# RWKV-6 with a SiLU MLP: a kernel's first unit turns its tokens in quarters of the array, spreads u from one row and copies level 1 in another order

## The chip, the cores and the metric

The kernel runs on one core of one Trainium2 chip. The metric is the device time of one execution in microseconds (us). Before the change the median of three runs is 566.68 us (566.24, 566.68 and 570.93). One execution was recorded by the hardware profiler: it took 566.43 us, of which 564.6 us lie between the first and the last instruction (its span). Times of single instructions below are counted from the start of that span.

Names of engines: PE is TensorE (PEld its weight load), DVE is VectorE, ACT is ScalarE, POOL is GpSimd, SP is SyncE. SPq and ACTq are the instruction queues of SP and ACT when they issue DMAs.

## What is computed

Batch 4, 8 heads, 768 tokens, head dimension 48; then an MLP from 384 to 2048 to 384. All data are float32.

```python
def _attn_ref(r, k, v, w, u):
    state = np.zeros((B, H, D, D))
    for t in range(S):
        kt, vt, rt, wt = k[:, :, t], v[:, :, t], r[:, :, t], w[:, :, t]
        cur = np.einsum('bhd,bhe->bhde', u[None] * kt, vt)
        y[:, :, t] = np.einsum('bhd,bhde->bhe', rt, state + cur)
        state = wt[:, :, :, None] * state + np.einsum('bhd,bhe->bhde', kt, vt)
    return y

def _moe_ref(x, w_in, w_out):          # x: (3072, 384), from y
    h = x @ w_in
    g = h * (1.0 / (1.0 + np.exp(-h)))
    return g @ w_out
```

A token's own key and value thus count with the weight u (the "bonus"), and older ones with the product of the decays w in between.

## The kernel before, in words

**Units.** The 768 tokens are cut into 6 stretches of 128 tokens (`L`), and the batch into pairs (`NB = 2`); one stretch of one pair is a unit, 12 in all. The order of the instructions on every engine is written out by hand: `do((fn, args), ...)` calls the steps one after the other, and each engine takes its own instructions in that order. The change touches the steps of unit 0 nearly alone; unit 1 shares some of its functions.

**Scores by levels.** Within a unit a 128 by 128 score matrix is built in 7 levels. Level l splits the tokens into blocks of `c = 2^l`: a query in an odd block meets the keys of the even block before it. For that, queries `tr`, keys `tk` and decays `tw` are needed with the head dimension on the partitions; between levels the queries and keys are multiplied on by products of decays (`grow_queries` on DVE, `grow_keys` on POOL, `product` mostly on POOL, `odd_keys` a copy on ACT). `score_products` on PE makes a level's scores in PSUM, and `keep_masked` (line 724 in the profile) copies them into `score` on DVE under a mask of int8, two copies of 128x512 for a level. At level 1 its pattern takes runs of two elements.

**First loads.** `load_tokens(0)` (line 111) fetches k, r and w of unit 0 into `raw`, each in two DMAs of 192 KB: the first batch element's tokens onto partitions 0 to 63 by SP's queue, the second's onto partitions 64 to 127 by ACT's queue. Each partition row holds two successive tokens. Behind them on SP's queue stand u, read once for every one of the 128 partitions (line 281), and the weights and later tokens.

**Turning.** `turn` (lines 357 to 390) brings tokens onto the columns with PE: a matmul by the identity. For each of the two tokens s of a row, `turn_in` issues 8 matmuls (4 head pairs p, 2 heads e) that contract over all 128 partitions; the 64-wide outputs of the two heads fill the upper and lower half of the PSUM partitions. An fp32 matmul stands in the trace as two instructions, so one `turn_in` shows as 16. `turn_out` copies the result into `tk`, `tr` or `tw` on ACT: for k in two copies of 128x256 (the second batch element reversed), else in one of 128x512. For w the order of s is reversed (`back`).

**Bonus.** `bonus(0, 0)` on POOL (line 442) multiplies r of a row's second token by k of its first; `bonus(0, 1)` on DVE (444) multiplies r by k of the same token, `bonus(0, 2)` (446) multiplies that by u, and `bonus_sum` (451, 455) reduces over the head dimension. `bonus_spread` brings the sums into place with PE, and `bonus_part(x)` (603) writes a quarter of them into `score`.

**First keys.** `start_keys(0, DVE, True)` and `(..., False)` (line 672) are four DVE products of 128x128 elements with steps of four elements. Behind them on DVE stand `grow_queries(0, 0)` (629) and `product(0, 0)` (416), and POOL's `grow_keys(0, 1)` (647) waits for the latter.

**Beats.** `beat(n)` issues n transposes of the identity on PE (line 1382) whose result nobody reads.

The DVE and ACT share the PSUM tile `p_w` of two banks for rounding the weights later on; in unit 0 the first bank takes the spread bonus, and the second is free.

Of the kernel before, what the change touches and what calls it, by code (L numbers as in the profile page):

```python
# [38 lines left out]
def kernel(  # L39
# [73 lines left out]

    def load_tokens(i):
        for name, src in (("k", k), ("r", r), ("w", w)):
            load_twos(twos(raw[:, i % NSLOT, WRK[name]])[0], src, i, [nc.sync, nc.scalar if i == 0 else nc.sync])

    def load_blocks(i, name, g):

# [152 lines left out]
    u_bc = const.tile([128, H, D], F32, name="u_bc")  # L272

    def load_u():
        for b in range(NB):
# [62 lines left out]
    own_mask = const.tile([128, NB, L // 2, 2], I8, name="own_mask")  # L338
    for b in range(NB):
        for x in range(2):  # L340
            nc.vector.tensor_single_scalar(out=own_mask[:, b, :, x:x + 1], in_=first[0], scalar=tok[:, x, b:b + 1],
                                           op=ALU.is_equal)
        for l in range(1, NL):
            nc.vector.tensor_single_scalar(out=masks[l][:, b], in_=first[l], scalar=tok[:, l, b:b + 1], op=ALU.is_equal)

    def clear_score():
        nc.gpsimd.memset(score, 0.0)
# [4 lines left out]
    def turn(i, b, name):  # L352
        dst = {"w": tw, "r": tr, "k": tk}[name]
        if i not in dst:
            rows = NX if name == "k" else Q
            t = pt.tile([128, rows, L], F32, name="t" + name, bufs=2 if name == "r" else 1)
            dst[i] = [t] if name == "w" else t
        t = dst[i][0] if name == "w" else dst[i]
        if i < NTOK:
            if (i, b, name) not in turned:  # L360
                turn_in(i, b, name)
# [9 lines left out]
    def turn_in(i, s, name):  # L371

        flat = raw[:, i % NSLOT, WRK[name]].rearrange("p b h d -> p (b h d)")
        p_tr = bank("p_sc" if (i, name) == (0, "r") else "p_m", NP, NB, L // 2)
        for p in range(NP):
            for e in range(2):
                at = ((2 * p + e) * 2 + s) * D
                nc.tensor.matmul(p_tr[PD * e:PD * e + PD, p].rearrange("p b i -> p (b i)"), lhsT=flat[:, at:at + PD],
                                 rhs=ident, start=(p == 0), stop=(p == NP - 1))
        turned[i, s, name] = p_tr  # L380

    def turn_out(i, s, name, t):
        p_tr = turned.pop((i, s, name))
        if name == "k":
            to = t[:, NP:].rearrange("p q (i s) -> p q i s", s=2)
            nc.scalar.copy(out=to[:, 0:NP, :, s], in_=p_tr[:, :, 0])
            nc.scalar.copy(out=to[:, NP:2 * NP, :, 1 - s], in_=p_tr[:, ::-1, 1, ::-1])
        else:
            to = t.rearrange("p (b q) (i s) -> p q b i s", b=NB, s=2)[:, :, :, :, s]
            nc.scalar.copy(out=to, in_=p_tr)  # L390

    def clear_rest():

# [34 lines left out]
    def bonus(i, x):  # L428
# [3 lines left out]
        if x == 0:  # L432
# [7 lines left out]
            if i == NTOK:  # L440
                ruk[i, 0] = spare[:, 0:H * D].rearrange("p (h d) -> p h d", h=H)
            engine.tensor_tensor(out=ruk[i, 0], in0=rk(i, 0)[:, :, 1], in1=rk(i, 1)[:, :, 0], op=ALU.mult)
# [222 lines left out]
    def start_keys(i, engine, own):  # L665

        n = NP * L // 4
        for b in range(NB):
# [3 lines left out]
            engine.tensor_tensor(out=keys(i, X[1] * L + 3 * b, [4, n], [1, 1]) if own else have, in0=have,  # L672
                                 in1=odd_products(i, 0, b, [4, n], skip=2 * x), op=ALU.mult)

    def start_levels(i):

        start_keys(i, nc.gpsimd, True)
# [43 lines left out]
    def keep_masked(i, l, e, sc):  # L721
        c, ni = 1 << l, L >> (l + 1)
        dst = score[:, i % NSC, e].rearrange("p (b q) (i s c) -> p b q i s c", b=NB, s=2, c=c)[:, :, :, :, 1, :]
        nc.vector.copy_predicated(out=dst, mask=masks[l][:, :, None].to_broadcast([128, NB, NP, ni, c]),  # L724
                                  data=sc[e].rearrange("p (b q) (i c) -> p b q i c", b=NB, c=c))

    def scores(i, l, *between):
        c, ni = 1 << l, L >> (l + 1)
# [665 lines left out]
    others = {1: [(beat, 6)], 2: [(turn, 1, 0, "r"), (head_weight, 0), (beat, 2), (bonus_part, 1)],  # L1394
              3: [(turn, 1, 1, "r"), (head_weight, 1), (beat, 2), (bonus_part, 2)], 4: [(turn, 1, 1, "w"), (reverse_v, 0), (bonus_part, 3)],
              5: [(turn, 1, 0, "w")], 6: [(turn_in, 1, 0, "k"), *blocks[0:4], (tail_weight, 0)]}
    for l in range(1, NL):
        do((scores, 0, l), *[(grow_keys, 0, l + 1)] * (l + 1 < NL), *others[l])

    do((bonus, 1, 0), (bonus, 1, 1), (product, 1, 0), (bonus, 1, 2), *both(x_products, 0), (join_weight, 0), (add_weight,),  # L1400
       (x_copy, 0, 0), (tail_weight, 1), (x_copy, 0, 1), (turn_apart, 0), (turn_in, 1, 1, "k"), *both(turn, 1, "k"), (join_weight, 1),
       (odd_ones, 1), (start_keys, 1, nc.gpsimd, True), (add_weight,), (tail_weight, 2), (head_weight, 2), (grow_queries, 1, 0),
       (up, 0, 0), (turn_k, 0), (join_weight, 2), *blocks[4:8],
       (start_keys, 1, nc.gpsimd, False), (add_weight,), (tail_weight, 3), (odd_keys, 1, 1), (head_weight, 3), (grow_keys, 1, 1),
# [93 lines left out]
```

## Time and profile before

| what | value |
|---|---|
| median of three runs | 566.68 us |
| profiled execution | 566.43 us, span 564.6 us |
| PE busy | 555.2 us (98%) |
| DVE busy | 477.3 us (85%) |
| POOL busy | 396.2 us (70%) |
| ACT busy | 272.0 us (48%) |
| PE busy from 5 to 65 us | 56.40 of 60 us |
| PE busy from 65 to 180 us | 114.99 of 115 us |
| PE's granted clock (page) | full in all 40 slices |
| DMA moved | 57.59 MB |

An engine's busy time is the time in which one of its instructions runs; a bracket such as [0.88 <-DVE tw L416] ahead of an instruction says how long its engine stood idle, and what ended that. In a line of the timeline "x32" stands for 32 instructions merged into one stretch. Matmuls overlap, so a matmul's own duration is longer than the distance to the next.

### The profile page before, as it was taken

The numbers are of one execution on the slowest core, as the hardware profiler recorded it, in microseconds if no ns is written. First come the engines' busy times: TensorE is split into PE (matmuls) and PEld (weight loads), VectorE is DVE, ScalarE is ACT, GpSimd is POOL, SyncE is SP. The second block draws the span as 40 slices with busy tenths as digits, with TensorE's granted clock in tenths as the row PEclk, the third lists the DMA queues.
The fourth block names the chain that finished last, engine by engine and source line by source line (L and its number), as shares of the span: only waits on it lengthen the run. The fifth ranks groups of instructions, "written<-read, shape, count | busy, mean of one in ns | idle before, by whom it ended". The sixth has DMA issues, their size and how long they took to land.

```text
span 564.6 us, 18890 instructions
## 1 busy us (share of the span) xinstructions
PE 555.2 (98%) x7782; PEld 516.8 (92%) x7782; DVE 477.3 (85%) x747; ACT 272.0 (48%) x618; POOL 396.2 (70%) x448
## 2 busy tenths in 40 slices
PE   8999999999999999999999999999999999999997
PEld 7777777699899989999999999999999999999997
DVE  7999798998999989999889889889889989882250
ACT  4679695452461372373374274274274272271330
POOL 6999898527789998969796696696696696700000
PEclk9999999999999999999999999999999999999999
DMA  9946886345445445265555554555555552102000
GB/s 221 311 80 189 241 252 106 46 78 116 104 76 87 106 78 96 56 133 95 106 96 97 118 87 90 118 86 92 115 84 97 115 88 61 39 4 57 29 9 21
DMA packets 206485, 57.59 MB, mean 102 GB/s; under 512 B 186048, under 2 KB 198208, under 8 KB 206400
## 3 DMA queue, kind: packets, MB, share of 16 engines
q1 hardware_dynamic: 203712, 54.23, 46.6%
q10 hardware_dynamic: 2688, 2.16, 1.6%
q8 instruction: 61, 1.00, 0.8%
q14 instruction: 24, 0.20, 0.1%
HBM read 47.14 MB, written 9.18 MB: 100 GB/s over the span
## 4 chain that ended last, share of the span: by engine, by line
PE 68%; POOL 12%; DVE 8%; DMA 4%; issue 3%; SPq 3%; ACT 1%; DVEq 0%; POOLq 0%
PE p_o L1339 22%; PE p_o L1193 13%; PE p_h L1193 9%; PE p_h L1086 4%; PE p_m L1275 4%; PE p_h L1339 4%; POOL tk L647 2%; PE p_sc L706 2%; PE p_sc L1339 2%; SPq L127 2%; POOL ruk L498 2%; PE p_m L870 2%; POOL tw L416 2%; POOL w_in_sb L1132 2%; DVE tr L629 2%
## 5 line engine op out<-in xcount | busy, mean ns | idle before, releaser
L647 POOL TENSOR_TENSOR tk<-tk,tw 128x256 f32<-128x256 f32 x112 | 88.6, 811 | 5.1 <-PE p_sc L706 1.5
L1339 PE MATMUL p_o<-own,temps 128*128 128x192 f32 x496 | 82.8, 326 | 0.0
L1339 PEld LDWEIGHTS p_o<-own,temps 128*128 128x128 f32 x496 | 80.9, 190 | 0.1
L1193 PE MATMUL p_o<-xt,w_in_sb 128*64 128x128 f32 x1152 | 72.3, 273 | 0.9 <-POOL w_in_sb L1132 0.7
L416 POOL TENSOR_TENSOR tw<-tw 128x256 f32<-128x256 f32 (+6 forms) x71 | 42.3, 595 | 38.2 <-DVE tw L366 34.8
L1086 PE MATMUL p_h<-xt,w_in_sb 128*128 128x256 f32 x288 | 66.3, 384 | 1.8 <-POOL w_in_sb L260 1.5
L1193 PEld LDWEIGHTS p_o<-xt,w_in_sb 128*64 128x64 f32 x1152 | 64.7, 137 | 1.3 <-POOL w_in_sb L1132 1.0
L1086 PEld LDWEIGHTS p_h<-xt,w_in_sb 128*128 128x128 f32 x288 | 53.5, 190 | 10.4 <-POOL w_in_sb L260 3.0
L498 POOL TENSOR_TENSOR ruk<-tokens_rk 128x384 f32<-128x384 f32 x48 | 54.3, 1152 | 9.3 <-DMA tokens_rk<-in_k_dram 9.3
L629 DVE TENSOR_TENSOR tr<-tr,tw 128x512 f32<-128x512 f32 x57 | 53.4, 937 | 1.1 <-PE p_m L706 0.4
L1339 PE MATMUL p_o<-w_out_sb,gt 128*128 128x192 f32 x292 | 51.7, 330 | 0.3 <-DVE ob L1347 0.3
L1339 PEld LDWEIGHTS p_o<-w_out_sb,gt 128*128 128x128 f32 x292 | 47.4, 190 | 1.5 <-DVE ob L1347 0.9
L656 POOL TENSOR_TENSOR tk<-tk,tw 128x256 f32<-128x256 f32 x32 | 25.1, 813 | 27.2 <-DVE tk L366 22.6
L1308 DVE TENSOR_TENSOR temps<-gt 128x512 f32<-128x512 f32 (+1 forms) x48 | 43.7, 948 | 0.0
L1344 ACT COPY partial<-p_o 128x192 f32<-128x192 f32 x32 | 10.2, 318 | 66.5 <-PE p_o L1339 64.7
L617 ACT COPY tk<-tk 128x256 f32<-128x256 f32 x52 | 20.9, 402 | 39.4 <-POOL tk L647 29.4
L1217 ACT ACTIVATE gt<-p_o 128x512 f32<-128x512 f32 x45 | 26.0, 602 | 23.1 <-PE p_o L1193 23.0
L1339 PE MATMUL p_h<-w_out_sb,gt 128*128 128x192 f32 x184 | 31.9, 326 | 0.0
L1339 PE MATMUL p_o<-w_out_sb,temps 128*128 128x192 f32 x176 | 30.5, 327 | 0.0
L1339 PEld LDWEIGHTS p_h<-w_out_sb,gt 128*128 128x128 f32 x184 | 30.2, 190 | 0.0
L724 DVE COPY_PREDICATED score<-mask,p_sc 128x512 f32<-128x512 int8 x38 | 28.4, 809 | 1.3 <-PE p_sc L706 1.3
L1339 PEld LDWEIGHTS p_o<-w_out_sb,temps 128*128 128x128 f32 x176 | 28.8, 190 | 0.3 <-ACT partial L1344 0.3
(258 smaller groups left out, 1314.6 us busy)
## 6 DMA issues: line engine op xcount, KB each, us to landing
w_out_sb<-in_moe_w_in_dram SPq DMA_DIRECT2D x6, 768.0 KB, 6.8
turned<-yt SPq DMA_DIRECT2D x18, 192.0 KB, 2.7
xt<-turned SPq DMA_DIRECT2D x9, 384.0 KB, 3.4
w_out_sb<-in_moe_w_out_dram SPq DMA_DIRECT2D x4, 768.0 KB, 5.4
own<-in_moe_w_out_dram SPq DMA_DIRECT2D x4, 768.0 KB, 5.6
tokens_w<-in_w_dram SPq DMA_DIRECT2D x8, 384.0 KB, 4.6
tokens_rk<-in_r_dram SPq DMA_DIRECT2D x7, 384.0 KB, 4.3
tokens_rk<-in_k_dram SPq DMA_DIRECT2D x7, 384.0 KB, 5.4
```

The costliest lines, as they stand in the source:

```text
L416: engine.tensor_tensor(out=up, in0=t[:, :, 0::2], in1=t[:, :, 1::2], op=ALU.mult)
L498: mul = lambda out, one, two: nc.gpsimd.tensor_tensor(out=out, in0=one, in1=two, op=ALU.mult)
L629: nc.vector.tensor_tensor(out=odd, in0=odd, in1=tw[i][l][:, :, 0::2][:, :, :, None].to_broadcast([128, Q, L >> (l + 1), c]), op=ALU.mult)
L647: nc.gpsimd.tensor_tensor(out=out, in0=have, in1=odd_products(i, l, b, *blocks), op=ALU.mult)
L656: nc.gpsimd.tensor_tensor(out=have, in0=have, in1=odd_products(i, l, b, [2, NP * ni]), op=ALU.mult)
L724: nc.vector.copy_predicated(out=dst, mask=masks[l][:, :, None].to_broadcast([128, NB, NP, ni, c]), data=sc[e].rearrange("p (b q) (i c) -> ...
L1086: nc.tensor.matmul(p_h[:, a, :], lhsT=w_in_sb[:, c, f * 128:(f + 1) * 128], rhs=xt[i][:, c, :], start=(a == 0 and c == 0), stop=(a == 1 an ...
L1193: nc.tensor.matmul(p[h:h + PD, q, :], lhsT=left[:, f:f + PD], rhs=right, start=first and q == 0, stop=q == 3, skip_group_check=True)
L1217: nc.scalar.activation(out=g(f, t), in_=have, func=AF.Silu)
L1275: nc.tensor.matmul(po[i, b], lhsT=gt[i, f // 2][:, f % 2, b * L:(b + 1) * L], rhs=w_out_sb[:, f, :], start=(f == 0), stop=(f == FC - 1))
L1308: nc.vector.tensor_tensor(out=out, in0=one, in1=two, op=op)
L1339: nc.tensor.matmul(p, lhsT=left(f), rhs=right[:, f, :], start=which in fresh and f == 0, stop=f == FH - 1, skip_group_check=True)
```

## The change

- The row of u is fetched once (1.5 KB) by ACT's queue, ahead of that queue's token loads; a matmul of a row of ones with it (`spread_u`) puts it on all 128 partitions of the second bank of `p_w`, and `copy_u` copies that to `u_bc` on ACT later. The 192 KB load of u on SP's queue is gone.
- Both halves of unit 0's w are loaded by SP's queue.
- `turn_in` works by batch element instead of by s: matmuls contract over the 64 partitions of one batch element and move 64 columns, and for unit 0 the matmuls of both elements alternate, 32 matmuls (64 instructions) for each of k, r and w. `turn_out` is then one copy of 128x512 for each batch element, for k too; the second copy of unit 0's w is DVE's.
- `bonus(0, 1)` becomes k by u (read from PSUM), and `bonus(0, 2)` multiplies by r.
- `start_both` makes unit 0's first keys in two products of 128x256 instead of four of 128x128.
- Level 1's mask is stored, and its copies run, with the order of the two inner dimensions exchanged: 32 blocks innermost, with steps of four elements in `score` and of two in PSUM, for units 0, 1 and 2.
- In the order of steps: 8 beats, the spread of u and 7 beats in place of 16 beats; the mirror copies behind them; the k by u product before POOL's; `bonus_sum(0, 1)` and then `(0, 0)` ahead of w's turn; `bonus_part(1)` moved from behind level 2 to behind level 1.

```diff
-            load_twos(..., [nc.sync, nc.scalar if i == 0 else nc.sync])
+            load_twos(..., [nc.sync, nc.scalar if i == 0 and name != "w" else nc.sync])
...
+    u_bc = const.tile([128, H, D], F32, name="u_bc")
+    nc.scalar.dma_start(out=u_bc[0:1].rearrange("x h d -> x (h d)"), in_=u.rearrange("h d -> (h d)")[None, :])
     load_tokens(0)
+    ones = spare[0:1, 0:L]
+    nc.vector.memset(ones, 1.0)
...
-    nc.sync.dma_start(out=u_bc, in_=u.partition_broadcast(128))
     load_weight(0)
...
-                masks[l] = const.tile([128, NB, ni, c], I8, name=f"mask{l}")
+                masks[l] = const.tile([128, NB, *((c, ni) if l == 1 else (ni, c))], I8, name=f"mask{l}")
...
+    u_row = p_w[:, 1, 0:H * D].rearrange("p (h d) -> p h d", h=H)
+    def spread_u():
+        nc.tensor.matmul(p_w[:, 1, 0:H * D], lhsT=ones, rhs=u_bc[0:1].rearrange("x h d -> x (h d)"), start=True, stop=True)
+    def copy_u():
+        nc.scalar.copy(out=u_bc, in_=u_row)
+    def turn_in(i, name, *rows):
         flat = raw[:, i % NSLOT, WRK[name]].rearrange("p b h d -> p (b h d)")
+        for b in rows:
+            turned[i, b, name] = bank("p_sc" if (i, name) == (0, "r") else "p_m", NP, 2, L // 2)
         for p in range(NP):
-            for e in range(2):
-                at = ((2 * p + e) * 2 + s) * D
-                nc.tensor.matmul(p_tr[PD * e:PD * e + PD, p]..., lhsT=flat[:, at:at + PD], rhs=ident, ...)
+            for s in range(2):
+                for e in range(2):
+                    for b in rows:
+                        half, at = slice(b * L // 2, (b + 1) * L // 2), ((2 * p + e) * 2 + s) * D
+                        nc.tensor.matmul(turned[i, b, name][PD * e:PD * e + PD, p, s], lhsT=flat[half, at:at + PD], rhs=ident[half, half], ...)
+    def turn_out(i, b, name, t):
+        p_tr = turned.pop((i, b, name))
+        row0 = b * NP + (NP if name == "k" else 0)
+        to = t[:, row0:row0 + NP].rearrange("p q (i s) -> p q s i", s=2)
+        copy = nc.vector.tensor_copy if (i, b, name) == (0, 1, "w") else nc.scalar.copy
+        copy(out=to, in_=p_tr[:, ::-1, ::-1, ::-1] if name == "k" and b == 1 else p_tr)
...
+        elif i == 0:
+            by = u_row[:, :, None, :].to_broadcast([128, H, 2, D])
+            engine.tensor_tensor(out=ruk[i], in0=rk(i, 1) if x == 1 else ruk[i], in1=by if x == 1 else rk(i, 0), op=ALU.mult)
...
+    def start_both(i, engine):
+        n = NP * L // 4
+        for b in range(NB):
+            at = (NP + b * NP) * L + b
+            out = [at, at + 2]
+            out[b] = X[1] * L + 3 * b
+            engine.tensor_tensor(out=keys(i, out[0], [out[1] - out[0], 2], [4, n], [1, 1]), in0=keys(i, at, [2, 2], [4, n], [1, 1]),
+                                 in1=odd_products(i, 0, b, [2, 2], [4, n]), op=ALU.mult)
...
+        data = sc[e].rearrange("p (b q) (i c) -> p b q i c", b=NB, c=c)
+        if l == 1:
+            dst, data = (t.rearrange("p b q i c -> p b q c i") for t in (dst, data))
...
-    do((make_spread,), (beat, 16), *both(turn, 0, "k"), (bonus, 0, 0), (bonus, 0, 1), (odd_ones, 0), *both(turn, 0, "r"),
-       (bonus_sum, 0, 0), (clear_score,), (clear_state,), (clear_rest,), (bonus, 0, 2), *back(turn, 0, "w"), (bonus_sum, 0, 1), (start_keys, 0, nc.vector, True),
-       (start_keys, 0, nc.vector, False), (grow_queries, 0, 0), (product, 0, 0, nc.vector), (odd_keys, 0, 1), (grow_keys, 0, 1),
+    do((beat, 8), (spread_u,), (beat, 7), (make_spread,), *both(turn, 0, "k"), (bonus, 0, 1), (bonus, 0, 0), (odd_ones, 0),
+       *both(turn, 0, "r"), (bonus, 0, 2), (bonus_sum, 0, 1), (bonus_sum, 0, 0), (clear_score,), (clear_state,), (clear_rest,),
+       *both(turn, 0, "w"), (copy_u,), (start_both, 0, nc.vector), (grow_queries, 0, 0), (product, 0, 0, nc.vector), (odd_keys, 0, 1), (grow_keys, 0, 1),
        (beat, 3), (bonus_spread, 0), (beat, 5), (bonus_part, 0))
-    others = {1: [(beat, 6)], 2: [(turn, 1, 0, "r"), (head_weight, 0), (beat, 2), (bonus_part, 1)],
+    others = {1: [(bonus_part, 1), (beat, 6)], 2: [(turn, 1, 0, "r"), (head_weight, 0), (beat, 2)],
```

More of the change, by code (lines that the diff above doesn't have):

```diff
@@ L115, in load_tokens @@
         for name, src in (("k", k), ("r", r), ("w", w)):
-            load_twos(twos(raw[:, i % NSLOT, WRK[name]])[0], src, i, [nc.sync, nc.scalar if i == 0 else nc.sync])
+            load_twos(twos(raw[:, i % NSLOT, WRK[name]])[0], src, i, [nc.sync, nc.scalar if i == 0 and name != "w" else nc.sync])
     def load_blocks(i, name, g):
@@ L271 @@
     nc.scalar.activation(out=warm, in_=zero, func=AF.Silu)
-    u_bc = const.tile([128, H, D], F32, name="u_bc")
     def load_u():
@@ L343 @@
         for l in range(1, NL):
-            nc.vector.tensor_single_scalar(out=masks[l][:, b], in_=first[l], scalar=tok[:, l, b:b + 1], op=ALU.is_equal)
+            nc.vector.tensor_single_scalar(out=masks[l][:, b], in_=first[l].rearrange("p i c -> p c i") if l == 1 else first[l],
+                                           scalar=tok[:, l, b:b + 1], op=ALU.is_equal)
     def clear_score():
@@ L360, in turn @@
             if (i, b, name) not in turned:
-                turn_in(i, b, name)
+                turn_in(i, name, *(range(NB) if i == 0 else (b,)))
             turn_out(i, b, name, t)
@@ L369 @@
     turned = {}
-    def turn_in(i, s, name):
+    u_row = p_w[:, 1, 0:H * D].rearrange("p (h d) -> p h d", h=H)
[4 more added lines that the diff above has]
+    def turn_in(i, name, *rows):
         flat = raw[:, i % NSLOT, WRK[name]].rearrange("p b h d -> p (b h d)")
-        p_tr = bank("p_sc" if (i, name) == (0, "r") else "p_m", NP, NB, L // 2)
+        for b in rows:
+            turned[i, b, name] = bank("p_sc" if (i, name) == (0, "r") else "p_m", NP, 2, L // 2)
         for p in range(NP):
-            for e in range(2):
-                at = ((2 * p + e) * 2 + s) * D
[L378 to L390, printed above, removed]
+            for s in range(2):
+                for e in range(2):
+                    for b in rows:
+                        half, at = slice(b * L // 2, (b + 1) * L // 2), ((2 * p + e) * 2 + s) * D
+                        nc.tensor.matmul(turned[i, b, name][PD * e:PD * e + PD, p, s], lhsT=flat[half, at:at + PD], rhs=ident[half, half],
+                                         start=(p == 0 and s == 0), stop=(p == NP - 1 and s == 1), skip_group_check=True)
+    def turn_out(i, b, name, t):
[4 more added lines that the diff above has]
+        copy(out=to, in_=p_tr[:, ::-1, ::-1, ::-1] if name == "k" and b == 1 else p_tr)
     def clear_rest():
```

8 lines of the change are left out of this document (4 added, 4 removed).

## The prediction

> **What bounds the kernel now.** I read the page first (PE 98% busy), then the chain of waits in order of time, to see what sets the pace where the change lies. It shows unit 0's start as one chain (start, length, what):
>
> ```profile
> 1.36 3.67 PE p_m L1382 x16
> 5.03 2.01 PE p_m L378 x32
> 7.04 1.77 PE p_sc L378 x32
> ...
> 9.49 1.11 PE p_m L378 x16
> ...
> 10.62 0.67 ACT tw L390
> ...
> 11.31 1.32 DVE tk L672 x4
> ...
> 13.16 0.69 DVE tw L416
> ...
> 14.01 1.90 POOL tk L647 x2
> ```
>
> The beats, three turnings on PE, a copy of w on ACT, first keys and product on DVE, then POOL. Between 8.78 and 9.49 PE stands still. The transfers issued in the first 4.2 us say why (KB, us from issue to landing):
>
> ```profile
> raw<-in_k_dram SPq DMA_DIRECT2D x1, 192.0 KB, 3.4
> raw<-in_k_dram ACTq DMA_DIRECT2D x1, 192.0 KB, 4.2
> raw<-in_r_dram ACTq DMA_DIRECT2D x1, 192.0 KB, 5.2
> raw<-in_w_dram ACTq DMA_DIRECT2D x1, 192.0 KB, 6.9
> ```
>
> ACT issued these three at 0.74, 1.51 and 2.45: k is complete at 4.94, r at 6.71, w at 9.35. The waits name ACT's copy at 9.46, but w had landed only 0.1 before.
>
> Third, POOL's timeline, which takes over at 14 us:
>
> ```profile
> 6.92 1.78 POOL L442 TENSOR_TENSOR tokens_rk<-raw 128x384 f32<-128x384 f32 x1 [3.08 <-DMA raw<-in_r_dram]
> ...
> 11.78 1.35 POOL L396 MEMSET raw<- 128x720 f32 x2
> 14.01 1.89 POOL L647 TENSOR_TENSOR tk<-tk,tw 128x256 f32<-128x256 f32 x2 [0.88 <-DVE tw L416]
> ```
>
> From r's landing to 13.13 POOL works without a pause, then waits 0.88 for DVE. Last, busy time by stretch (PE, PEld, DVE, ACT, POOL):
>
> ```profile
> 25.00:45.00 20.00, 18.33 (x252) 14.56 (x249) 17.28 (x21) 16.25 (x29) 20.00 (x19) 1.00 0.64 166
> 45.00:60.00 15.00, 14.58 (x182) 11.81 (x181) 14.54 (x22) 13.90 (x22) 13.53 (x18) 1.00 0.67 191
> 65.00:180.00 115.00, 114.99 (x1155) 96.98 (x1154) 103.71 (x142) 58.24 (x129) 84.18 (x88) 1.00 0.54 112
> ```
>
> POOL is full to 45, PE from 65 on. So what POOL gains at 14 us reaches PE, and PE's full queue carries it to the end; what DVE gains beyond POOL is covered by POOL.
>
> **The change part by part.**
>
> *Loads.* u's row ahead of ACT's queue costs one issue: 0.43 (the shortest, L211) to 0.74 (k's own). I take 0.5, since it is one small transfer. k is then complete at about 5.45 and r at 7.2. w's second half goes behind its first on SP's queue, ahead of the weights and without u's 192 KB. Adding up the DMA rates by half microseconds, k's 0.39 MB had been moved by 3.9 (landed 4.94, a lag of 1.0) and the 1.18 MB of six token loads' size by 7.1. So w could land at 8.1; the other end is no gain, 9.35. I take 8.1: the traffic that stood between was u and the first weights. SP issues as many transfers as before.
>
> *Beats and u.* A beat takes 3.67/16 = 0.229. Eight end at 3.2; u's row lands 2.3 to 2.5 after its issue at 0.74 (as transfers of 32 and 16 KB, L127), thus 3.04 to 3.24; at worst like k, 4.13, a wait of 0.9. The spread is 2 instructions of 384 columns, six beats' worth; with 15 beats 21 in place of 16. In the trace matmuls drop from 418 to 272 ns at 5.05; the last five then cost 0.145 each (x6 in 0.87, L1382 at 14.5). The queue ends at 5.03 + 0.7 = 5.75, after k.
>
> *Turning.* 64 instructions of 64 columns on four quarters. The nearest row is level 6's scores (L706, 48x64 in quarters, x32 in 0.69 at 26.31): 1.38 for k instead of 2.05 (the other end, if the quarters ran two at a time). k: 5.75 to 7.15; ACT copies 128x512 twice (0.62 each, 0.5 apart) to 8.3, before 7.80. r: 7.2 to 8.6, copies to 9.75. w: after r on PE, the banks free at 8.3, landed 8.1: 8.6 to 10.0. Its copies run on ACT and DVE at once, to 10.7; before the second ended at 12.13. A change of tile shape on PE I cost at nothing: the 0.4 by which DVE's product comes ahead of POOL below covers it; without that cover it would add its whole length.
>
> *DVE.* k by u at 5.75 (0.96, L444; waits for u's spread, nothing due is queued behind it), times r 7.2 to 8.2, sums to 9.2, the POOL product's sum at 9.0 + 0.55, so 9.75: free before w's copy at 10.0, cover 0.25. First keys: 4 x 0.33 = 1.32 before; two of 256 lie between 0.84 (0.33 for 128 and 0.60 for 512, interpolated) and 1.32. I take 1.0, to 11.7. Queries 0.6 and product 0.7: done at 13.0 instead of 13.85. `copy_u` (0.48, L406) lies on ACT ahead of `odd_keys`, which waits for the keys at 11.7 anyway: nothing.
>
> *POOL.* Its run from 6.92 to 13.13 starts with r, now 7.2, and ends at 13.4; `odd_ones` needs k's copies at 8.3 and comes at 9.0. `grow_keys` starts at max(13.4, 13.0) = 13.4 instead of 14.01: **0.6 gained**, and r's later landing becomes the limit.
>
> *Level 1.* Two copies take 2.46, other levels' 1.31; six copies in units 0 to 2 change their order. Ends: 0.62 each as other levels (0.6 gained per copy) and 1.56 (four times L672's 0.39 for 128 elements, whose steps are 16 bytes as the new order's are in `score`): 0.33 lost. I take 1.23, unchanged, as nothing shows which operand makes them slow; `bonus_part(1)` ahead of level 2 costs nothing, as DVE's sum stays. In unit 0 DVE runs 0.4 ahead of POOL, in unit 2 PE is full; in unit 1 (37 to 40 us) POOL is full, but at 50.6 and 54.4 it waits 1.16 and 0.24 for ACT and DVE. Of that I take 0.1.
> [...]
>
> *Sum.* 566.43 - 0.6 - 0.1 = 565.7 for the profiled execution. The median lies 0.25 above that execution, so I predict **565.9**.
>
> **The rivals.**
>
> *Level 1 becomes fast and is worth it* (18 in 100). At 0.62, unit 1 gains 1.2 on DVE at 40, and the waits of 1.4 around 52 shrink with it, as POOL there waits for ACT and DVE, which are 93% and 97% busy. 0.6 + 1.4 = 2.0 gained: 564.7. Against it: ACT's share of the wait isn't touched.
>
> *The gain is absorbed* (15). w lands at 9.35 after all: PE 9.35 to 10.75, copies to 11.4, product done at 13.75, 0.1 gained; or SP's issues at 27 to 60 us set the pace. 566.6.
>
> *Slower: PE stays slow through the turnings* (12). The matmuls' drop from 418 to 272 ns came after 3.67 us of unbroken beats. The spread uses one row of the array and may wait for u; if the count starts anew behind it (about 4.6), the drop comes at 8.3. Then 21 beats end at 6.2, k at 8.5 (1.38 x 229/137), r at 9.9, w at 11.3, product at 14.25: 0.4 lost, 567.1. Slow through w's turn as well: r 10.8, w 13.1, product 16.0, 2.1 lost, 568.8. It decides from a drop at about 8.0 on; before that the product still beats 13.85. For it: the cover is thin. Against: beats stand on both sides.
> [...]
>
> [...] Level 1 at 1.56 costs DVE 0.66 in each unit: in unit 0 it eats DVE's lead and 0.3 of the 0.6, in unit 1 it adds as much to full engines: 566.7.
>
> *The forecast itself* (50), own range 565.3 to 566.4.
>
> **How the numbers follow.** The range leaves out the far end of the slow rival and takes in the fast one: 564.4 to 567.8. Over 1% (5.7 us, about what a measurement of this kernel can tell from no change) would need more than twice all that lies ahead of 14 us as waits and level 1 together (0.9 + 6 x 0.6 = 4.5), and the slow rival's worst is 2.1: faster 0.02, slower 0.03 for what no view shows, within 0.95.
>
> **What would show each step.** In the changed profile: u landing by 3.3 and no gap of PE between the beats; L378's new matmuls x64 in about 1.4 and at 272 ns or less; w landed near 8.1; DVE's product ending near 13.0; POOL's first `grow_keys` near 13.4 with no wait for DVE, but a later start at r; level 1's two copies at 2.46 or 1.25. Wrong would be a POOL that starts at 14 or later, DVE waiting for PE at 10 for over 1 us, or a start that is 0.6 earlier with an end that isn't.

## The result and the profile after

| | before | after |
|---|---|---|
| median | 566.16 us (6 runs, 565.57 to 570.93) | 584.02 us (6 runs, 582.04 to 584.59) |
| ratio | | 1.0296, 95% interval 1.0259 to 1.0334: **slower** |
| span of the profiled execution | 564.6 us | 582.2 us |
| mean granted clock of TensorE | 1.000 | 0.971 (0.971 to 0.982 in all six) |

The forecast was 565.9 us. Where executions of one kernel were granted different clocks, both kinds are given below. The page of the changed kernel shows the reason in one row that I had taken for constant. These are PE's busy share and its granted clock in tenths, in 40 slices of 14.6 us:

```profile
PE   8999899999999999999999999999999999999997
...
PEclk9559899999999999999999999999999999999999
```

The second and third slices ran at about half the clock, the fifth at 0.8 to 0.9. PE's busy row hides it: from 25 to 45 us PE was busy 20.00 of 20 us at a clock of 0.50. The stretches that the prediction shows of the kernel before now read (PE, PEld, DVE, ACT, POOL, then granted clock, DMA share, GB/s):

```profile
25.00:45.00 20.00, 20.00 (x244) 16.72 (x245) 10.48 (x15) 9.04 (x18) 12.40 (x14) 0.50 0.50 120
45.00:60.00 15.00, 12.51 (x167) 9.97 (x164) 13.16 (x14) 10.46 (x16) 9.74 (x11) 1.00 0.63 172
65.00:180.00 115.00, 114.05 (x1210) 92.55 (x1212) 104.88 (x138) 65.23 (x132) 85.80 (x88) 1.00 0.53 116
```

From 25 to 45 us PE is now full at half clock, and POOL, full before, has 12.40 of 20. In finer stretches the clock falls at about 14.3 us, comes back at 45, and halves once more from 62.1 to 65.5. A mean of 0.971 over 582 us is 0.029 x 582 = 16.9 us at full clock, nearly the whole 17.6 by which the spans differ. Following the same work through both traces shows where it was lost (start in us):

| work | before | after | behind |
|---|---|---|---|
| unit 0, second level's scores on PE | 15.95 | 19.45 | 3.5 |
| unit 0, first scores in quarters (48x64) | 26.31 | 38.29 | 12.0 |
| unit 1, the same | 36.23 | 50.62 | 14.4 |
| first MLP block of 36 matmul instructions | 68.99 | 86.29 | 17.3 |
| end | 564.6 | 582.2 | 17.6 |

Nearly all of it, 17.3 of 17.6 us, is lost in the first 86 us. PE's timeline says what came ahead of the fall at 14.3 (start, length, work, and idle time before it):

```profile
1.36 1.97 PE L1408 MATMUL p_m<-ident 128*128 128x128 f32 x8 [1.36 <-POOL ident masks.py:199]
3.26 1.64 PE L378 MATMUL p_w<-u_bc,spare 1*128 1x384 f32 x2
4.83 1.75 PE L1408 MATMUL p_m<-ident 128*128 128x128 f32 x7
6.52 1.99 PE L393 MATMUL p_m<-ident,raw 64*64 64x64 f32 x64
8.28 1.93 PE L393 MATMUL p_sc<-ident,raw 64*64 64x64 f32 x64
9.99 1.53 PE L393 MATMUL p_m<-ident,raw 64*64 64x64 f32 x64
12.24 0.55 PE L1408 MATMUL p_m<-ident 128*128 128x128 f32 x3 [0.73 <-ACT tw L401]
...
13.53 0.31 PE L1408 MATMUL p_m<-ident 128*128 128x128 f32 x1
15.02 1.01 PE L1408 MATMUL p_m<-ident 128*128 128x128 f32 x4 [1.18 <-issue]
15.96 2.08 PE L738 MATMUL p_h<-tr,tk 48*128 48x128 f32 x16
```

The spread of u stands between the beats with no gap, as planned. The turnings then take 1.99, 1.93 and 1.53, as their matmuls drop from 311 to 218 ns only at 10.8 (before, the drop from 418 to 272 came between 5.0 and 5.2; the array is called warm below from this drop on). Behind them PE stands still 0.73 for a copy, and 1.18 for nothing the profile names ("issue"). From there on x16 of scores take 2.08 us where they took 1.18; in the profile of before the same scores are

```profile
13.38 1.18 PE L714 MATMUL p_h<-tr,tk 48*128 48x128 f32 x16
```

POOL's timeline and one DMA row answer to those of before:

```profile
8.02 1.78 POOL L453 TENSOR_TENSOR tokens_rk<-raw 128x384 f32<-128x384 f32 x1 [4.18 <-DMA raw<-in_r_dram]
...
14.86 1.44 POOL L661 TENSOR_TENSOR tk<-tk,tw 128x256 f32<-128x256 f32 x2 [0.57 <-DVE tw L427]
```

```profile
raw<-in_r_dram ACTq DMA_DIRECT2D x1, 192.0 KB, 5.8
```

ACT issued this transfer at 2.04, so r is complete at 7.84 instead of 6.71. POOL's product starts with it, at 8.02 instead of 6.92, and POOL starts `grow_keys` 0.85 later than before instead of 0.6 earlier. Last, DVE's level 1, two copies, before and after:

```profile
15.22 2.46 DVE L724 COPY_PREDICATED score<-mask,p_h 128x512 f32<-128x512 int8 x2
...
18.70 4.72 DVE L751 COPY_PREDICATED score<-mask,p_h 128x512 f32<-128x512 int8 x2
```

That they take twice as long has nothing to do with PE's clock: in level1_alone below the pair takes 4.75 us while the clock is full.

### The profile page after: what moved, and what is told of

Its sections match the earlier page's. It is cut to its first block, busy times and chain, and to the rows that moved or that the text cites. A ratio compares the mean times of both kernels' runs of the same rounds, so it can differ in the third digit from the quotient of the medians.

```text
span 582.2 us, 19272 instructions
## 1 busy us (share of the span) xinstructions
PE 569.9 (98%) x7975; PEld 528.6 (91%) x7975; DVE 484.3 (83%) x747; ACT 272.0 (47%) x614; POOL 396.1 (68%) x448
## 3 DMA queue, kind: packets, MB, share of 16 engines
q10 hardware_dynamic: 2162, 1.97, 1.3%
## 4 chain that ended last, share of the span: by engine, by line
PE 79%; DVE 9%; POOL 4%; DMA 3%; issue 3%; ACT 2%; SPq 0%; DVEq 0%; POOLq 0%; ACTq 0%
PE p_o L1365 23%; PE p_o L1219 14%; PE p_h L1219 9%; PE p_h L1112 8%; PE p_h L1365 4%; PE p_sc L730 3%; DVE score L751 2%; PE p_m L896 2%; PE p_m L393 2%; PE p_sc L1365 2%; PE p_m L1301 2%; PE p_m L875 1%; PE p_m L730 1%; DVE p_w L247 1%; DVE tr L643 1%
## 5 line engine op out<-in xcount | busy, mean ns | idle before, releaser
L1112 PE MATMUL p_h<-xt,w_in_sb 128*128 128x256 f32 x288 | 68.0, 391 | 1.4 <-POOL w_in_sb L260 1.4
L643 DVE TENSOR_TENSOR tr<-tr,tw 128x512 f32<-128x512 f32 x57 | 51.9, 910 | 9.9 <-PE p_h L738 5.6
L512 POOL TENSOR_TENSOR ruk<-tokens_rk 128x384 f32<-128x384 f32 x48 | 52.7, 1118 | 6.5 <-DMA tokens_rk<-in_k_dram 6.5
L1334 DVE TENSOR_TENSOR temps<-gt 128x512 f32<-128x512 f32 (+1 forms) x48 | 42.1, 915 | 0.0
L1370 ACT COPY partial<-p_o 128x192 f32<-128x192 f32 x32 | 10.2, 320 | 67.3 <-PE p_o L1365 67.3
L751 DVE COPY_PREDICATED score<-mask,p_sc 128x512 f32<-128x512 int8 x38 | 35.4, 1005 | 0.3 <-PE p_sc L730 0.3
L512 POOL TENSOR_TENSOR ruk<-ruk,u_bc 128x384 f32<-128x384 f32 x16 | 29.5, 1862 | 0.0
```

The lines of the kernel that those rows point to most:

```text
L512: mul = lambda out, one, two: nc.gpsimd.tensor_tensor(out=out, in0=one, in1=two, op=ALU.mult)
L643: nc.vector.tensor_tensor(out=odd, in0=odd, in1=tw[i][l][:, :, 0::2][:, :, :, None].to_broadcast([128, Q, L >> (l + 1), c]), op=ALU.mult)
L1112: nc.tensor.matmul(p_h[:, a, :], lhsT=w_in_sb[:, c, f * 128:(f + 1) * 128], rhs=xt[i][:, c, :], start=(a == 0 and c == 0), stop=(a == 1 an ...
L1334: nc.vector.tensor_tensor(out=out, in0=one, in1=two, op=op)
```

## The experiments

The first theories, in words: **Q**, the quarter turning causes the slow clock; **L**, level 1's copies cause it by making PE wait; and that the spread of u, one row of the array, delays the warm-up. In each diff "-" is the kernel that the run starts from.

**old_turn**: the changed kernel with the turning of before.

```diff
-        for b in rows: ... matmul(..., lhsT=flat[half, at:at + PD], rhs=ident[half, half])   # 64 columns, 64 partitions
+        nc.tensor.matmul(p_tr[PD * e:PD * e + PD, p], lhsT=flat[:, at:at + PD], rhs=ident)    # 128 columns
```

> The changed kernel with the turning of before (matmuls over all 128 partitions, 128 columns, 96 instead of 192 matmul instructions in unit 0). Theory Q (the quarters load the array too little and use up PE's instructions too fast, so that its clock rises late and falls again): the matmuls reach 272 ns before 8 us, no fall of the granted clock at 14 us, mean clock above 0.99, time 566 to 570 with level 1 still at 2.4 us a copy. Theory L (the dear copies of level 1 hold PE up, and that lets the clock fall): the clock still falls, time 580 or more. Theory S (the spread with one row of the array spoils the warm-up): rise at about 10 us as in the changed kernel, and a fall at 14 is likely, time above 575.

576.85 us (576.69 to 577.63; before in the same session 565.64), ratio 1.0201 [1.0181, 1.0221], clock 0.991 to 0.993; the time lies between what Q (566 to 570) and L (580 or more) asked for. The drop to fast matmuls comes at 7.65, and nothing falls at 14. But PE then waits for DVE, which is busy with level 1:

```profile
23.28 1.16 PE L740 MATMUL p_h<-tr,tk 48*128 48x128 f32 x16 [2.76 <-DVE tr L645]
```

and the clock is 0.68 from 25 to 30 us, and 0.71 and 0.60 from 50 to 60, behind unit 1's level 1. So Q explains the long slow stretch, and L is a second cause.

**old_level1**: the changed kernel with level 1 of before.

```diff
-        if l == 1:
-            dst, data = (t.rearrange("p b q i c -> p b q c i") for t in (dst, data))
```

> The changed kernel with level 1's mask and copies of before. Theory Q: the copies go back to 1.25 us each, but the clock still falls at 14 us, before the first of them; mean clock 0.97 to 0.985, time 577 to 583. Theory L: the clock stays at 1, time 565 to 567. Theory S: as Q.

580.42 (579.68 to 580.54), 1.0257 [1.0237, 1.0277], clock 0.973. Two copies take 2.44 again; the clock falls at 14.1 all the same. With the copies at their old price 14.8 us of loss are left: level 1 is the smaller part here.

**beats_first**: the spread behind 16 unbroken beats.

```diff
-    do((beat, 8), (spread_u,), (beat, 7), (make_spread,), ...
+    do((beat, 16), (spread_u,), (make_spread,), ...
```

> The changed kernel with 16 unbroken beats first and the spread of u behind them (instead of 8, the spread, 7). Theory S: the matmuls drop to 272 ns near 5 us as before, the turnings run warm, the clock doesn't fall at 14 us, time 566 to 572. Theory Q: early rise perhaps, but the fall comes all the same behind the quarters, time above 575. Theory L: 580 or more.

582.63 (582.05 to 582.76), 1.0297 [1.0277, 1.0317], clock 0.974. The drop came at 9.1 instead of 10.8 and w's turning took 1.29, but the clock fell at 16.1, behind a pause of 2.08 of PE. A warm-up that comes this much earlier recovers nothing that can be told from no change.

**level1_alone**: before, with level 1's order alone.

```diff
+        if l == 1:
+            dst, data = (t.rearrange("p b q i c -> p b q c i") for t in (dst, data))
```

> The kernel of before with level 1's new order alone (mask and copies). Copies of 2.4 to 2.7 us instead of 1.25, six of them. Theory Q and S: granted clock stays at 1, time 567 to 570 (1.2 to 1.4 us more for each of four copies in units 0 and 1, those of unit 2 covered by PE, part of unit 1's covered by POOL). Theory L: the clock falls, 575 or more.

574.43 (570.5 at clock 1.0; 574.43 and 575.16 at 0.990), 1.0136 [1.008, 1.0192]. DVE and PE in unit 0:

```profile
14.89 4.75 DVE L728 COPY_PREDICATED score<-mask,p_h 128x512 f32<-128x512 int8 x2
```

```profile
20.31 1.16 PE L715 MATMUL p_h<-tr,tk 48*128 48x128 f32 x16 [2.13 <-ACT temps L230]
```

DVE's next product starts only at 19.27, and PE waits behind it; the view names ACT, as that came last. The windows from 20 to 30 show 0.71 and 0.61. One part of the change by itself thus slows the copies and, in two of three executions, by the wait they cause, PE.

**level1_filled** keeps PE busy through those waits: 14 beats behind unit 0's level 1 and 18 in unit 1, added to level1_alone.

```diff
-2: [(turn, 1, 0, "r"), ...
+2: [(beat, 14), (turn, 1, 0, "r"), ...
...
-       (up, 0, 2))
+       (up, 0, 2), (beat, 18))
```

> Level 1's new order alone in the kernel of before, with 14 beats in the stretch where PE waits for it in unit 0 and 18 in unit 1 (they compute nothing that is read). Theory I: the clock stays at 1, and what is left is the copies' own price, time 567 to 570.5. Rival (the clock falls because the score matmuls themselves load it too little, or the loss is the copies' own): clock falls as without the beats, 573 or more.

571.43 (571.08 to 571.47; before 566.48), 1.009 [1.0062, 1.0117], clock 1.000 in all three. The beats, which compute nothing, made it faster than level1_alone at 0.990: the fall of the clock hung on PE's pause. What is left, 5.0 us, is the copies' own price at full clock: four copies of units 0 and 1, each 1.15 dearer, are 4.6. The one execution of level1_alone at clock 1.0, which has no such beats, was 4.9 behind its own before. I had expected less, as POOL was to cover DVE. It waits too:

```profile
21.63 1.67 POOL L648 TENSOR_TENSOR tk<-tk,tw 128x256 f32<-128x256 f32 x2 [2.20 <-PE p_h L715]
```

**level1_psum** asks which operand makes the copies dear. In level1_alone the copy steps by four elements in `score` and by two in PSUM; here PE writes unit 0's scores in the copy's order, so that PSUM is read without steps.

```diff
-    ap=[r_p.ap[0], [apart * L, 2], [2 * c, ni], [1, c]]
+    ap=[r_p.ap[0], [apart * L, 2], *([[1, c], [2 * c, ni]] if (i, l) == (0, 1) else [[2 * c, ni], [1, c]])]
```

> Level 1's new order alone in the kernel of before; in unit 0 PE writes level 1's scores into PSUM in the order in which the copy reads them (columns of the queries taken with steps of four), so that the copy steps in the score tile alone; units 1 and 2 as in the change. Theory P (the steps of two elements in PSUM make the copies dear): unit 0's copies 1.3 us or less, unit 1's 2.4. Theory M (the steps of 16 bytes in the score tile do): 2.4 in both. If both count, something between, near 1.8. The time falls by what unit 0's copies save, and by unit 0's fall of the clock (574.4 to about 569 to 571) under P, and stays under M.

575.54 (575.08, 576.0; before 565.98), 1.0166 [1.0149, 1.0184], clock 0.991. Unit 0's copies:

```profile
16.46 4.74 DVE L729 COPY_PREDICATED score<-mask,p_h 128x512 f32<-128x512 int8 x2
```

4.74 against 4.75: PSUM's steps cost DVE nothing, and the steps of 16 bytes in `score` are what is left.

**quarters_alone**: before, with the quarter turning alone (w's second copy on DVE with it).

> The kernel of before with the turning in quarters alone (16 beats, no spread, u loaded as before). Theory I: PE's 96 further instructions use up what was fetched, PE stands behind its 220th matmul or so for 1 to 2 us until about 15 us, and the clock falls at 12 to 16 us: 575 to 582. Rival (only spread and quarters together delay the rise and bring the fall): clock 1, time 565 to 567.

577.9 (577.21 to 578.32; before 566.48), 1.0204 [1.0175, 1.0233], clock 0.973 to 0.976. PE's timeline:

```profile
1.36 3.28 PE L1381 MATMUL p_m<-ident 128*128 128x128 f32 x16 [1.36 <-POOL ident masks.py:199]
5.00 1.16 PE L381 MATMUL p_m<-ident,raw 64*64 64x64 f32 x64 [0.35 <-DMA raw<-in_k_dram]
6.78 1.16 PE L381 MATMUL p_sc<-ident,raw 64*64 64x64 f32 x64 [0.62 <-DMA raw<-in_r_dram]
8.26 1.28 PE L381 MATMUL p_m<-ident,raw 64*64 64x64 f32 x64 [0.31 <-DMA raw<-in_w_dram]
10.25 0.55 PE L1381 MATMUL p_m<-ident 128*128 128x128 f32 x3 [0.71 <-ACT tw L389]
11.34 1.21 PE L586 MATMUL p_w<-own_sums,partial 128*128 128x16 f32 x8 [0.54 <-DVE own_sums L454]
12.40 0.53 PE L1381 MATMUL p_m<-ident 128*128 128x128 f32 x3
13.57 0.44 PE L1381 MATMUL p_m<-ident 128*128 128x128 f32 x2 [0.64 <-issue]
```

Here the array is warm in time, and a turning takes 1.16 to 1.28, better than the 1.38 I had reckoned with. What it saves becomes idle time of PE: 0.35, 0.62, 0.31, 0.71, 0.54 and 0.64, together 3.17 us of the 9.5 ahead of the fall, and from about 14.3 to 41.7 us the clock is 0.50. In the same 9.5 us the kernel before is idle for 0.76. No single pause is longer than 0.71: here short gaps among small tiles were enough.

What keeps the clock down is a second matter. Here it is 0.50 for 27.3 us with PE busy throughout. In spread_behind_k (below), with the turning of before, it is back after 6.8 us of a PE just as busy (stretch, its length, PE, PEld, DVE, ACT, POOL, clock, DMA share, GB/s; quarters_alone first):

```profile
14.35:41.66 27.31, 27.31 (x312) 22.80 (x310) 16.03 (x21) 11.08 (x22) 18.09 (x23) 0.50 0.75 196
...
15.03:21.86 6.83, 6.83 (x52) 5.39 (x48) 6.38 (x8) 1.39 (x4) 5.99 (x9) 0.50 0.97 281
```

In every profile that has such stretches in its first 100 us they last one, two, eight or nine times 3.41 us: one or two in the kernels with the old turning, and eight or nine in unit 0 of the changed kernel, old_level1, beats_first, no_beats_behind and here, which all turn in quarters. In these five the clock comes back 2.6 to 4.7 us after the first products of scores and values (matmuls on 128 rows, from 38.09 here). My reading is that at half clock the quarters and the 48-row scores did not bring it back, though PE was busy 27.31 of 27.31 us. No run tries that by itself.

**quarters_filled**: the same with two 128x512 matmuls, which nobody reads, in place of five beats behind the turnings.

```diff
-       (beat, 3), (bonus_spread, 0), (beat, 5), (bonus_part, 0))
+       (fill,), (beat, 3), (bonus_spread, 0), (fill,), (bonus_part, 0))
```

> The turning in quarters alone in the kernel of before, with PE kept at full-array work behind w's turn: two matmuls of 128x512 in place of the 5 beats (one ahead of the 3 beats, one behind the bonus' spread); nothing reads them. Theory I (PE loses its clock because it is idle or lightly loaded there, not because of the quarters themselves): granted clock 1, time 565.5 to 567.5, against 577.9 without them. Rival (matmuls on quarters count too little for the clock, whatever is around them): the clock falls near 14 us all the same, above 574.

Three executions at a clock of 0.999 to 1.0 took 567.61, 567.65 and 568.24, two at 0.997 took 570.33 and 572.06, one at 0.976 took 578.46 (before 565.91); the ratio over the other five is 1.0037 [1.0003, 1.0072]. Filling the idle time gives back most of the 11.4 us of quarters_alone. At full clock the faster turning with its fillers is still no gain: 1.7 to 2.3 us behind before. What these are is not shown; in the profile the second filler, from 13.83 to 14.93, stands right ahead of the first scores at 15.05. The profile is of the execution of 572.06 us, and it has a long pause of its own, behind which the clock halved from 32.5 to 35.9:

```profile
31.80 0.21 PE L705 MATMUL p_sc<-tr,tk 48*64 48x64 f32 x1 [3.08 <-issue]
```

**old_turn_old_level1**: the changed kernel with both parts undone; the loads, the spread and the steps' order are left.

> The changed kernel with both the turning and level 1 of before; left of the change are u's row and its spread, w on one queue, the product of k by u first, the keys in two products and the order of steps. Theory I (any stretch in which PE stands or is lightly loaded for some 2 us out of 3.4 halves its clock; quarters and dear copies each make one): no such stretch is left, granted clock 1 throughout, time 566 to 568.5, up to 2 us more than before as r lands 1.1 later and the rise comes at 7.6. Rival (the spread or the loads are by themselves enough to let the clock fall): mean clock below 0.995, time above 570.

571.86 (568.88 and 569.04 at clock 1.0; 571.86 to 572.24 at 0.994; before 566.48), 1.0075 [1.0042, 1.0107]. The third part costs 2.4 to 2.6 us at full clock and 5.4 to 5.8 at 0.994. In the profiled execution the drop comes at about 10.6, and the clock is 0.50 from 17.6 to 24.4: theory I ruled that fall out, and it came in three of five executions. The figures of that theory lie near those of the changed kernel (1.91 us of idle time, 0.73 and 1.18, between 11.5 and 15.0; one slow stretch of 3.4, from 62.1 to 65.5), but no run shows its threshold: quarters_filled was idle for 2.08 of 3.7 us, from 6.5 to 10.2, and its clock stayed up until 32.5.

**no_beats_behind**: old_level1 without the eight beats behind the turnings. It was to tell whether the pause marked "issue" belongs to the beats.

> The changed kernel with level 1 of before and without the 3 and 5 beats behind w's turn. If PE's pause before 15 us is the fetch of instructions (it came behind the 221st matmul in three kernels), it now comes 8 matmuls further on, in the midst of the score matmuls of level 1 (behind their 4th instruction), and ends at about 14.7 to 15.2 all the same. If it is a wait for data, the scores start as soon as the queries are there (13.9) and run through. Clock falls in both, time 579 to 583.

579.21, clock 0.976, one execution.

```profile
13.62 0.50 PE L737 MATMUL p_h<-tr,tk 48*128 48x128 f32 x4 [0.54 <-DVE tr L642]
15.91 1.66 PE L737 MATMUL p_h<-tr,tk 48*128 48x128 f32 x12 [1.80 <-issue]
```

The pause has moved into the middle of one group of scores, behind its fourth matmul, and again the view names no data that PE waited for. Counted from the start it stands behind PE's 221st matmul instruction, as in the changed kernel, in old_level1 and in beats_first; in quarters_alone it is the 222nd. Ahead of it the queue of instructions moves one packet of 16 KB (61 packets and 1.00 MB in the whole kernel before): at 12 to 13 us in the changed kernel (the pause ends at 15.02), at 13 to 14 here (15.91), at 10 to 11 in quarters_alone (13.57). So PE seems to run out of fetched instructions there. Before, the packet also comes at 13 to 14, but the 222nd matmul is due only at about 21. The quarters issue 96 more matmul instructions in unit 0, and that is what brings the point forward. The pause of 3.08 in quarters_filled stands behind the 473rd, 252 further on. That fetching is the cause is inferred from count and packet, not seen directly.

**spread_behind_k** and **mended**: repairs. Both have the old level 1, 16 beats, and the spread behind k's turning; the first has the old turning, the second the quarters with the two fillers.

```diff
-    do((beat, 8), (spread_u,), (beat, 7), (make_spread,), *both(turn, 0, "k"), (bonus, 0, 1), ...
+    do((beat, 16), (make_spread,), *both(turn, 0, "k"), (spread_u,), (bonus, 0, 1), ...
```

> The changed kernel with the turning and level 1 of before, 16 unbroken beats and the spread of u behind k's turn. Theory I (the spread with one row of the array between the beats delays the rise, and that is what was left of the loss): the rise comes at 4.2 to 5.3 us again, clock 1, time 565.5 to 567.5 against 571.9. Rival (r landing later, as its DMA stands behind u's row and beside w on SP's queue, costs the rest): rise early, but 568 to 570.

> The changed kernel with level 1 of before, 16 unbroken beats, the spread behind k's turn, quarters, and the two 128x512 matmuls that fill PE behind w's turn. Theory I: clock 1, the start as the change meant it, 564.5 to 567. Rival (quarters or fetch still open a gap): clock below 0.99, above 572.

spread_behind_k: 568.98 (568.39 and 568.48 at clock 1.0, 569.48 and 569.65 at 0.994; before 565.91), 1.0057 [1.0039, 1.0075]; k's turning took 1.97, so the array was warm by 5 us. mended: 568.37 at clock 1.0, and 579.19, 579.42 and 580.63 at 0.973 to 0.976: one kernel, two outcomes. The pause is there in the execution at full clock too:

```profile
14.45 0.29 PE L600 MATMUL p_w<-own_sums,partial 128*128 128x16 f32 x2 [2.07 <-issue]
```

so even 2.07 us of it don't always bring the clock down. And at full clock neither repair reaches the kernel before.

**loads_old**: spread_behind_k with the loads in the order of before. Theory R: r's late landing is what costs these 2.5 us.

```diff
-    nc.scalar.dma_start(out=u_bc[0:1]..., in_=u...)
     load_tokens(0)
+    nc.sync.dma_start(out=u_bc[0:1]..., in_=u...)
```

> As spread_behind_k (turning and level 1 of before, 16 beats, spread behind k's turn), and the loads in the order of before: w's second half on ACT's queue again, u's row on SP's queue behind the tokens. Theory R (r lands 0.4 to 1.1 us later in every kernel that has u's row ahead on ACT's queue and both halves of w on SP's, and POOL's unbroken run starts with r): POOL's product starts at 6.8 to 7.2 instead of 7.8, first grow_keys at 13.9 to 14.4 instead of 15.0, time 566 to 567.5 against 569.0. Rival (the product of k by u waiting for the spread, and the order of steps, are what is left): no change, 568.4 to 569.7.

568.85 (568.55 to 568.97, all at clock 1.0; before 565.98), 1.0047 [1.0034, 1.006]. POOL could start on r at 6.57 in place of 7.83, and nothing was gained, as DVE now waits for the spread behind k, and POOL for DVE:

```profile
9.01 0.95 DVE L457 TENSOR_TENSOR tokens_rk<-raw,p_w 128x768 f32<-128x768 f32 x1 [3.45 <-PE p_w L377]
```

```profile
16.07 1.89 POOL L662 TENSOR_TENSOR tk<-tk,tw 128x256 f32<-128x256 f32 x2 [2.74 <-DVE tw L428]
```

R is not enough by itself: with u moved through PE, k by u hangs on PE's order, and what hangs on it reaches POOL.

**product_first** tests the premise of my sum, that what POOL gains at 14 us reaches the end. It is the kernel before, with one exchange on DVE.

```diff
-    (grow_queries, 0, 0), (product, 0, 0, nc.vector),
+    (product, 0, 0, nc.vector), (grow_queries, 0, 0),
```

> The kernel of before with the product of decays ahead of the first growing of queries on DVE, which POOL waits 0.88 us for at 14 us. Theory (POOL sets the pace from 14 to 45 us): POOL starts at 13.2 to 13.4 instead of 14.0, and 0.3 to 0.7 us come off, 565.2 to 565.6. Rival (level 1's scores on PE start 0.6 later instead, DVE's chain is as long, and PE's longer pause lets the clock fall in some executions): no gain, 565.7 to 567, with single executions above 570.

567.39 (five at clock 1.0: 566.72 to 567.86; two at 0.994: 568.58 and 569.24; before 565.98), 1.0032 [1.0019, 1.0046].

```profile
14.67 1.05 DVE L629 TENSOR_TENSOR tr<-tr,tw 128x512 f32<-128x512 f32 x1 [0.72 <-PE p_h L714]
```

```profile
12.87 1.73 POOL L647 TENSOR_TENSOR tk<-tk,tw 128x256 f32<-128x256 f32 x2
...
20.11 1.67 POOL L647 TENSOR_TENSOR tk<-tk,tw 128x256 f32<-128x256 f32 x2 [0.72 <-PE p_h L714]
...
22.77 1.65 POOL L647 TENSOR_TENSOR tk<-tk,tw 128x256 f32<-128x256 f32 x2 [0.79 <-PE p_sc L714]
...
25.98 1.45 POOL L442 TENSOR_TENSOR tokens_rk<-raw 128x384 f32<-128x384 f32 x1
```

POOL's `grow_keys` starts at 12.87, 1.14 earlier than before, without a wait (0.36 of it because r landed earlier in this execution). By 25.98 it is 0.41 later than before (25.57): its gain turns into waits for PE, which waits for DVE's queries. The 0.88 of POOL's wait that I set out to win was worth nothing here. The exchange also puts the first queries behind the product, so it doesn't show what POOL's start alone would be worth.

## Why the prediction was wrong

**The steps that failed**, by weight:

- *"A change of tile shape on PE I cost at nothing."* This is the step that failed. The sum priced PE's instructions; PE's idle time and its clock were not in it. The quarters took no longer than I said (1.16 to 1.28 in a warm array), but the time they save stands idle (3.17 us in 9.5 where it was 0.76), the clock halves, and in quarters it took 27.3 us to come back (6.8 in spread_behind_k). quarters_alone lost 11.4 us without any other part; with the idle time filled it was 1.7 to 2.3 behind in half of its executions.
- *The slow rival's price, 2.1 at worst.* It named the right thing, a slow PE through the turnings: the drop came at 10.8, far beyond its 8.0, and the product was done at 14.7. But I let PE stay fast once it was fast. The clock fell 3.5 us after the matmuls' drop (10.8 and 14.3), and stayed down 30.7 us. quarters_alone, warm before 5 us, shows that an early rise doesn't prevent that.
- *Level 1, ends 0.62 and 1.56, taken at 1.23.* It took 2.4 to 2.7, outside both ends. The row for the upper end (L672's products, steps of four too) doesn't carry over to a predicated copy. The rival that had level 1 at 1.56 (5 in 100) had the sign that I discounted, and too low a price. In `score` the runs show 0.65 a copy with four or more elements in a row, 1.23 with two, 2.4 with one in each 16 bytes. In PSUM they show no price of steps: 4.74 for two copies without, 4.75 with.
- *"What DVE gains beyond POOL is covered by POOL", and what it loses too.* level1_filled shows 5.0 us at full clock for 4.6 of dearer copies: nothing was covered. product_first points the same way: 1.14 earlier on POOL gave nothing. My reading of this is that in units 0 and 1 DVE, PE and POOL form a ring (queries, scores, copies, keys), and that POOL's full rows were one view of that ring and not its limit.
- *The absence of anything large.* A change of over 1%, 5.7 us, was to need "more than twice all that lies ahead of 14 us as waits and level 1 together", which I put at 4.5. That is wrong in its own numbers, as 5.7 is 1.3 times 4.5, and a change in PE's clock for 30 us was not in the sum. With the clock open, 0.03 for slower was far too low.

**Terms that were off.** r was complete at 7.84 instead of 7.2 (POOL's start in the changed load order: 7.35 to 8.02 in all runs, against 6.56 to 7.24): the row of u did take 0.52 to issue, but the transfer from r's own issue took 5.8 where it had taken 5.2 (5.1 to 5.8 in the profiles of the changed load order, 4.1 to 5.2 in those of the old one). First keys took 1.20 instead of 1.0. w was to land at 8.1; in the changed kernel PE came to it too late to tell, but in mended it waited for w until 9.23.

**Steps that held.** u landed by 3.26 and the beats had no gap. A turning in the warm array was at or below 1.38. The absorbed gain, a rival at 15 in 100, comes nearest to the executions at full clock, but they are worse than its 566.6: 567.6 to 569.0 in quarters_filled, spread_behind_k, loads_old and old_turn_old_level1, all 1.7 to 3.0 us above the kernel before. What these last microseconds are stays open.

**How the loss divides.** Level 1 alone costs 8.8 (5.0 its own, the rest clock), the quarters alone 11.4, the rest 2.4 to 5.8. That is up to 26.0 and more than the 17.9 measured: the parts share one slow stretch, and in the changed kernel level 1's first waits fall where the clock is at half already. No version tried is faster than the kernel before.

**What stays open.** What PE has to do, and for how long, to keep its clock. quarters_filled stood idle 2.08 between 6.5 and 10.2 us without losing the clock at once; quarters_alone lost it in each of its three executions; mended went either way. Busy time alone does not decide it. In two stretches of 3.41 us, the length of the shortest slow one, the first of quarters_filled, which kept the clock, the second of quarters_alone, which lost it at the end, PE was busy

```profile
8.62:12.03 3.41, 1.85 (x64) 1.34 (x64) 2.06 (x3) 1.38 (x3) 3.41 (x5) 1.00 1.16 287
...
10.94:14.35 3.41, 2.36 (x19) 1.89 (x21) 3.41 (x9) 0.45 (x1) 2.33 (x6) 1.00 1.23 233
```

The first holds most of a 128x512 filler, the second eight matmul instructions of 16 columns. Why the slow stretches last whole multiples of 3.41 us, and why one kernel (mended) had two outcomes, no run shows. Nor was the fetch of instructions tried by itself.

## What to carry to other kernels

Where PE sets the pace, read its granted clock before and after, and price a faster PE step by the idle time that it leaves. In quarters_alone 3.17 us of saved PE time, in pauses of at most 0.71, were followed by 27.3 us at half clock; with matmuls that compute nothing in the pauses (quarters_filled) five of six executions ran at 0.997 to 1.0, and one at 0.976. Small matmuls may also keep the clock from coming back: the slow stretch took 27.3 us with the quarters and 6.8 with the old turning (spread_behind_k). Split into many small matmuls, work seems to bring forward a point at which PE must wait for instructions (a pause of 0.64 to 1.80 us behind the 221st or 222nd matmul instruction, which is due at about 21 us in the kernel before, began at about 13 to 14 in quarters_alone, the changed kernel and no_beats_behind), so count them. In a predicated copy look at the neighbours in each 16 bytes of SBUF (two copies of 128x512 took 1.31 us with four, 2.46 with two, 4.7 with one), and look for the price of one in that operation, not in another with the same steps.

## What the runs showed of the hardware

- In quarters_alone PE's clock was halved behind six pauses of 0.31 to 0.71 us (3.17 of 9.5 us) and stayed at 0.50 for 27.3 us; in the changed kernel, behind pauses of 0.73 and 1.18, for 30.7. PE was busy there: 20.00 of 20 us from 25 to 45 in the changed kernel, mostly with 48-row and 64x64 matmuls. With the old turning the slow stretches of the first 100 us lasted 3.4 or 6.8 us (24.8 to 28.2 in old_turn, 15.03 to 21.86 in spread_behind_k).
- The page's granted clock reads full in the first 10 us even where matmuls are slow: 311 ns until 10.8, 218 after, in the changed kernel. Only the durations show the change there.
- The rise to fast matmuls came between 4.1 and 7.2 us in the kernels with 16 unbroken beats and no spread ahead of the first turning, and between 7.6 and 10.8 in those with the one-row spread among the beats or right behind them. What else moves it within these ranges stays open.
- Two predicated copies of 128x512 into SBUF take 1.31, 2.46 or 4.7 to 4.8 us with four or more, two or one element in a row in each 16 bytes.
- PE's level 1 scores took 2.07 instead of 1.18 us for x16 when their queries were read with steps of 16 bytes (level1_psum), at full clock.
